# Layer two's last stage of a two-layer network on one core: where factor loads are issued, and how many places the squares have

## The chip, the core and the metric

The kernel runs on one core of a Trainium2 chip. TensorE multiplies, VectorE and ScalarE prepare its operands and empty its accumulators, and 16 DMA engines move data between HBM and the core's memory. Transfers are issued from two queues here: SyncE's (written SP) and ScalarE's (written ACT). The metric is device time of the whole program in microseconds (us), lower is better.

## What is computed

A causal attention with decaying weights feeds two layers; the change touches the last matrix product of the second layer.

```
x = attention(q, k, v)                     # 2304 tokens x 512
h1 = x @ w_in1;  g1 = elu(h1);  y = g1 @ w_out1
h2 = maximum(y @ w_in2, 0)                 # 2304 x 2048
out = (h2 * h2) @ w_out2                   # 2304 x 512
```

All weights arrive as 64-bit floats and everything must hold float32 accuracy. So each operand is split into a high and a low part, and each product is three matmuls (high by high, high by low, low by high).

## The kernel before, in words

Both products of layer two are done as Strassen-like products: the matrices are cut into 2x2 blocks, and seven block products replace eight. For `(h2*h2) @ w_out2` the seven combinations of the weight blocks, the **factors**, are made earlier in the program and parked in HBM (`wo2s`); the squares `h2*h2` are parked in HBM too (`g2s`).

The stage of the second product (`up2`, matmuls of line 492) works through steps numbered `i` = 0 to 23; its matmuls write accumulators A, B and D, ScalarE copies or squares them (lines 509, 570, 571), VectorE adds (lines 519, 522), and SyncE stores the squares (line 525).

The last stage (`down2`, matmuls of line 675) follows. Its unit is called a **set** here: for one column of 128 tokens per half (`u`, nine of them) and one pair of feature blocks (`jj`, four of them), it loads 512 KB of squares from `g2s` (line 637, queue SP), makes seven combinations out of them, splits each (a cast on ScalarE in line 159, a subtraction on VectorE in line 160; sums between blocks on VectorE in lines 659 and 662), and runs 7 products x 2 blocks x 3 = 42 matmuls. There are 36 sets, 1512 matmuls. The first call takes `u` = 0 and 1 by turns, so set 0 is (jj 0, u 0), set 1 is (jj 0, u 1), set 2 is (jj 1, u 0), set 3 is (jj 1, u 1), set 4 is (jj 2, u 0) and so on to set 7; after that four sets for each `u`.

The loaded squares go to the pool `raw`, three places of 512 KB, taken in rotation; the load of a set waits until the set three before it has been cast and summed. The split combinations `S` go to three places in rotation (two of pool `x`, one made of four tiles of pool `g`).

The factors come back from HBM in ten **groups** of six tiles, 1536 KB each (the tenth 512 KB), by `load_last` in line 615, issued from ScalarE's queue. The group takes the memory that the operands T of the second product held (tags `w0` to `w9`), so it waits until these are used. Groups 0 to 4 are issued after the steps that the dictionary in line 874 names, 5 to 9 in the first five passes of `down2`, right behind the issue of a set's load of squares (line 642). For the 42 matmuls of set 0 or 1 the groups 0 to 2 are needed, for sets 2 and 3 the groups 2 to 4, for sets 4 and 5 the groups 4 to 6, for sets 6 and 7 the groups 7 to 9; from then on all ten stay in memory.

What is issued on an engine follows an order that a scheduler makes with a model of times, starting from the order of the program; each engine's queue is then worked off strictly in that order. In the trace the sets' squares are tiles `g` (in the order below `g_7052` is set 0, `g_7111` set 1, `g_7170` set 2, `g_7232` set 3, `g_7291` set 4), and the groups are tiles `wo` (`wo_6957` is group 3, `wo_7023` group 4, `wo_7054` group 5, `wo_7113` group 6, `wo_7172` group 7, `wo_7234` group 8, `wo_7293` group 9).

Of the kernel before, what the change touches and what calls it, by code (L numbers as in the profile page):

```python
# [9 lines left out]
F32 = mybir.dt.float32  # L10
# [8 lines left out]
P = 128  # L19
# [53 lines left out]
def tokens(half, u):  # L73

    blk = max(b for b in range(NB) if COL0[b] <= u * P)
    t, n = BLOCKS[blk]
    return t + half * n // 2 + u * P - COL0[blk]
# [49 lines left out]
def tile_kernel(ctx: ExitStack, tc, q, k, v, w_in1, w_out1, w_in2, w_out2, cst, out):  # L127
# [3 lines left out]
    wp = pool("wp", 1)  # L131
    raw_p = pool("raw", 3)
# [24 lines left out]
    def split(pair_hi, pair_lo, src, eng=nc.vector):  # L157

        nc.scalar.copy(pair_hi, src)  # L159
        eng.tensor_tensor(out=pair_lo, in0=src, in1=pair_hi.bitcast(F32), op=ALU.subtract)  # L160
# [213 lines left out]
    def down(blk, f):  # L374
        n = BLOCKS[blk][1]
        g, w = g_t.pop((blk, f)), w_t[0, 1, f]
        shared = blk < 2
        first, last = (any(f == r[e] - (e == 1) for r in (GROUPS if shared else ((0, NF),))) for e in range(2))
        if first:
            acc_t[blk] = [ps_acc.tile([P, TB], F32, tag="acc", name=f"acc{m}") for m in range(KC)]  # L380

        back = shared and last and f >= GROUPS[0][1]
        end = last and f == NF - 1
        part = []
        for m in range(KC if last else 0):
            if end:
                if m % 2 == 0:
                    both = raw_p.tile([P, 2, TB], F32, tag="raw", name="x2")
                t = both[:, m % 2]
            else:  # L390
                t = n_p.tile([P, TB], F32, tag="qkv"[m % 3], name="part")
            part.append(t[:, :n])
            if back:
                nc.sync.dma_start(out=part[m], in_=parts[blk, :, m, :n])
        for m in range(KC):
            c = slice(m * P, (m + 1) * P)
            a = acc_t[blk][m][:, :n]
            mm3(a, w[:, 0, c], w[:, 1, c], g[:, 0, :n], g[:, 1, :n], first, last)
            if not last:
                continue  # L400
            if back:
                nc.vector.tensor_tensor(out=part[m], in0=a, in1=part[m], op=ALU.add)  # L402
            else:
                nc.scalar.copy(part[m], a)
            if not end:
                nc.sync.dma_start(out=parts[blk, :, m, :n], in_=part[m])
                continue
            for half in range(2):
                for j in range(n // 2 // P):
                    o = half * n // 2 + j * P  # L410
                    nc.sync.dma_start(
                        out=x2s[COL0[blk] // P + j][:, m // 2 * 2 + half, m % 2], in_=part[m][:, o:o + P]
                    )
# [197 lines left out]
    def load_last(g):  # L611
        t = wp.tile([P, 6, 2, DM // 2], F32R, tag=f"w{g}", name=f"wo{g}")
        n = min(6, 7 * HF - 6 * g)

        tc.keep_in_program_order(nc.scalar.dma_start(
            out=t.bitcast(F32)[:, :n].rearrange("p q a b -> p q (a b)"),
            in_=wo2s[6 * g:6 * g + n].rearrange("q p a b -> p q (a b)"),
        ))
        for i in range(n):
            wo_t[6 * g + i] = t[:, i]  # L620

    sets = [0]

    def down2(us, loads=()):

        loads = list(loads)
        banks = {}
        for i, u in enumerate(us):
            for k in range(4):
                ps, tag = ((ps_acc, "acc"), (ps_acc, "acc"), (ps_h, "h"), (ps_a, "a"))[k]  # L630
                banks[u, k] = ps.tile([P, 2, DM // 2], F32, tag=tag, name=f"m{k}")
        m = lambda u, k: banks[u, PLACE[k][0]][:, PLACE[k][1]]
        for jj in range(HF // 2):
            for u in us:
                c, s = divmod(u, NCH)
                r = raw_p.tile([P, 2, 4, P], F32, tag="raw", name="g2")
                nc.sync.dma_start(
                    out=r.rearrange("p j x c -> p j (x c)"),
                    in_=g2s[c][s, 2 * jj:2 * jj + 2].rearrange("j p a b c -> p j (a b c)"),
                )  # L640
                if loads:
                    load_last(loads.pop(0))

                if sets[0] % 3 < 2:
                    t = x_p.tile([P, 2, 2, 7, P], F32R, tag="x", name="S")
                    at_ = [t[:, :, :, o] for o in range(7)]
                    span = lambda o, n: t[:, :, :, o:o + n]
                else:
                    ts = [g_p.tile([P, 2, 2, 2, P], F32R, tag="g", name="S") for _ in range(4)]
                    at_ = [ts[(o + 1) // 2][:, :, :, (o + 1) % 2] for o in range(7)]  # L650
                    span = lambda o, n: ts[(o + 1) // 2][:, :, :, (o + 1) % 2:(o + 1) % 2 + n]
                sets[0] += 1
                a11, a21, a12, a22 = (r[:, :, i] for i in range(4))

                def put(o, n, src):
                    d = span(o, n)
                    split(d[:, :, 0], d[:, :, 1], src)

                sub = lambda out, x, y: nc.vector.tensor_tensor(out=out, in0=x, in1=y, op=ALU.subtract)  # L659
                put(0, 1, r[:, :, 0:1])  # L660
                put(1, 2, r[:, :, 2:4])
                nc.vector.tensor_tensor(out=a22, in0=a21, in1=a22, op=ALU.add)
                sub(a21, a11, a21)
                sub(a11, a22, a11)
                sub(a12, a12, a11)
                put(3, 2, r[:, :, 0:2])
                put(5, 2, r[:, :, 2:4])
                for k in (1, 2, 6, 7, 4, 5, 3):
                    for e in range(2):
                        j = 2 * jj + e  # L670
                        l, w = at_[ST[k - 1]][:, e], wo_t[7 * j + WT[k - 1]]
                        for i, (x, y) in enumerate(((0, 0), (0, 1), (1, 0))):

                            first = j == 0 and i == 0
                            ins = nc.tensor.matmul(  # L675
                                m(u, k), l[:, x], w[:, y], start=first and k in (1, 6, 4, 5), stop=j == HF - 1 and i == 2,
                                skip_group_check=True,
                            )
                            if first:
                                tc.stamp_issue_order_token(ins.ins, f"bank{u}_{PLACE[k][0]}")  # L680
        for u in us:
            c1 = n_p.tile([P, DM], F32, tag="q", name="c1")
            v = n_p.tile([P, DM], F32, tag="k", name="v")
            o = [n_p.tile([P, 2, DM // 2], F32, tag="v", name=f"o{h}") for h in range(2)]
            c1, u2, u3 = c1[:, :DM // 2], v[:, :DM // 2], v[:, DM // 2:]
            add = lambda out, x, y: nc.vector.tensor_tensor(out=out, in0=x, in1=y, op=ALU.add)
            nc.scalar.copy(c1, m(u, 1))
            add(o[0][:, 0], m(u, 2), c1)
            add(u2, m(u, 6), c1)
            add(u3, m(u, 7), u2)  # L690
            add(o[1][:, 0], m(u, 4), u3)
            add(o[1][:, 1], m(u, 5), u3)
            add(u2, m(u, 5), u2)
            add(o[0][:, 1], m(u, 3), u2)
            for h in (1, 0):
                t0 = tokens(h, u)
                nc.sync.dma_start(out=out[t0:t0 + P, :], in_=o[h].rearrange("p a b -> p (a b)"))
# [154 lines left out]
    def expand(n):  # L852
        make(n)
        first, *rest = made[n]
        queue[0:0] = rest + [lambda: make(n + 1)]
        first()

    for i, (f, c) in enumerate(seq):
        now = up2(f, c)
        for n, (at_, _) in enumerate(tasks):  # L860
            if at_ == i:
                if i in (5, 18):
                    queue.extend([lambda: None] * 2)
                queue.append(lambda n=n: expand(n))
        for k in TURNS.get(i, (1, 5, 7, 2, 6, 4, 3)):
            whose = last if k in (7, 4) else now
            if whose:
                whose[k]()
            if k in (7, 4) and pend:
                down(*pend.pop(0))  # L870
            between()
        last = now

        for g in {20: (0,), 21: (1, 2), 22: (3,), 23: (4,)}.get(i, ()):
            load_last(g)
    while queue:
        queue.pop(0)()
    last[7]()
    last[4]()
    down2((0, 1), (5, 6, 7, 8, 9))  # L880
    for u in range(2, NU):
        down2((u,))

# [25 lines left out]
```

## Time and profile before

| | us |
|---|---|
| median of 3 runs | 890.87 |
| lowest and highest run | 886.36, 891.96 |
| profiled execution, whole time | 890.54 |
| its span (first to last instruction) | 888.7 |
| TensorE busy in the span | 857.8 (97%) |
| VectorE, ScalarE busy | 685.7, 490.6 |

The three runs lie 5.6 us apart, so one run says little about a few us. The profiled execution lies 0.33 us under the median, with 1.84 us around its span. All times of single instructions below come from this one execution, counted from the start of the span; the last stage runs from about 696 to 885.

### The profile page before, as it was taken

The page shows a single profiled execution, that of the slowest core. Times are in us where ns is not written, and L with a number is a line of the kernel's source. Part 1 is how long each engine was busy: PE and PEld are TensorE (multiplying, and loading weights), DVE is VectorE, ACT ScalarE, POOL GpSimd, SP SyncE. Part 2 cuts the span into 40 slices and gives each one's busy share as a digit, 9 for nine tenths or more (in the row PEclk, how much of TensorE's full clock was granted, in tenths as well). Part 3 has the DMA queues.
Part 4 walks back from the last instruction along what each step waited for, and adds up shares of the span by engine and source line. Part 5 has one row for each costly group of instructions (what it writes and reads, how often), then busy time and mean ns, then how long its engine had stood idle before and what let it go on. Part 6 is the DMA issues. An engine that isn't in the chain of part 4 may idle for free.

```text
span 888.7 us, 14956 instructions
## 1 busy us (share of the span) xinstructions
PE 857.8 (97%) x5630; PEld 771.3 (87%) x5630; DVE 685.7 (77%) x1391; ACT 490.6 (55%) x961; POOL 8.7 (1%) x12
## 2 busy tenths in 40 slices
PE   7898999999998999999999999999999989999998
PEld 5686888888887988888888898999989989999997
DVE  4998888885666868766778867789884769898984
ACT  3674778673464656555767744556553434444441
POOL 3000000000000000000000000000000000000000
PEclk9999899999999999999999999999999999999999
DMA  9944306383529656533462034499998994444330
GB/s 226 276 107 160 96 24 190 119 214 95 142 63 221 163 157 185 187 107 131 142 225 95 25 104 157 154 328 332 348 319 281 401 345 137 160 146 144 120 131 37
DMA packets 157608, 155.33 MB, mean 175 GB/s; under 512 B 62816, under 2 KB 121312, under 8 KB 157536
## 3 DMA queue, kind: packets, MB, share of 16 engines
q1 hardware_dynamic: 150208, 139.69, 51.9%
q10 hardware_dynamic: 7328, 14.68, 4.6%
q8 instruction: 44, 0.72, 0.3%
q14 instruction: 28, 0.23, 0.1%
HBM read 98.77 MB, written 55.57 MB: 174 GB/s over the span
## 4 chain that ended last, share of the span: by engine, by line
PE 73%; DVE 10%; DMA 9%; issue 3%; ACT 2%; SPq 2%; ACTq 0%; DVEq 0%
PE m L675 18%; PE acc L163 7%; PE acc L164 7%; PE acc L165 7%; PE h L163 7%; PE h L164 6%; PE h L165 6%; PE A L492 5%; PE D L492 3%; DMA k<-in_k_dram 2%; DMA f<-w2s 2%; PE ps_o L325 2%; DVE go L519 1%; DMA wo2s<-wo 1%; PE ps_o L321 1%
## 5 line engine op out<-in xcount | busy, mean ns | idle before, releaser
L675 PE MATMUL m<-wo,S 128*128 128x256 f32 x1512 | 183.8, 284 | 3.6 <-ACT S L159 3.6
L675 PEld LDWEIGHTS m<-wo,S 128*128 128x128 f32 x1512 | 183.3, 193 | 4.0 <-ACT S L159 4.0
L159 ACT CAST S<-g 128x512 fp32r<-128x512 f32 (+1 forms) x144 | 75.3, 565 | 94.2 <-DVE g L659 45.6
L163 PE MATMUL h<-x,w 128*128 128x512 f32 (+1 forms) x320 | 120.3, 378 | 3.4 <-DVE t L370 2.4
L165 PE MATMUL h<-x,w 128*128 128x512 f32 (+1 forms) x320 | 118.8, 371 | 0.0
L164 PE MATMUL h<-x,w 128*128 128x512 f32 (+1 forms) x320 | 118.7, 371 | 0.0
L164 PE MATMUL acc<-g,w 128*128 128x512 f32 (+1 forms) x320 | 118.5, 371 | 0.0
L165 PE MATMUL acc<-g,w 128*128 128x512 f32 (+1 forms) x320 | 117.5, 370 | 0.0
L492 PE MATMUL A<-T,pair 128*128 128x384 f32 x576 | 113.4, 336 | 1.5 <-DVE go L519 0.8
L163 PE MATMUL acc<-g,w 128*128 128x512 f32 (+1 forms) x320 | 111.4, 375 | 2.2 <-DVE x L402 1.3
L492 PEld LDWEIGHTS A<-T,pair 128*128 128x128 f32 x576 | 100.5, 188 | 4.0 <-DVE go L519 2.3
L160 DVE TENSOR_TENSOR S<-g,S 128x512 fp32r<-128x512 f32 (+1 forms) x144 | 86.4, 621 | 22.7 <-ACT S L159 20.9
L365 ACT ACTIVATE t<-h 128x512 f32<-128x512 f32 (+1 forms) x80 | 44.3, 554 | 82.5 <-PE h L165 78.9
L369 DVE SCALAR_TENSOR_TENSOR t<-e,t 128x512 f32<-128x512 f32 (+1 forms) x80 | 50.8, 635 | 49.3 <-ACT t L367 49.0
L163 PEld LDWEIGHTS h<-x,w 128*128 128x128 f32 x320 | 60.6, 190 | 15.5 <-DVE t L370 3.4
L159 ACT CAST g<-t 128x512 fp32r<-128x512 f32 (+1 forms) x80 | 46.2, 578 | 47.0 <-DVE t L370 45.2
L163 PEld LDWEIGHTS acc<-g,w 128*128 128x128 f32 x320 | 59.4, 188 | 13.4 <-DVE x L402 1.7
L165 PEld LDWEIGHTS h<-x,w 128*128 128x128 f32 x320 | 60.7, 190 | 10.6 <-DVE w L160 0.2
L164 PEld LDWEIGHTS h<-x,w 128*128 128x128 f32 x320 | 60.7, 190 | 10.2
L164 PEld LDWEIGHTS acc<-g,w 128*128 128x128 f32 x320 | 60.3, 188 | 10.2
L165 PEld LDWEIGHTS acc<-g,w 128*128 128x128 f32 x320 | 60.2, 188 | 10.1
L492 PE MATMUL D<-T,pair 128*128 128x384 f32 x288 | 58.5, 336 | 1.7 <-DVE pair L160 1.1
(88 smaller groups left out, 1279.3 us busy)
## 6 DMA issues: line engine op xcount, KB each, us to landing
g2s<-go SPq DMA_DIRECT2D x48, 384.0 KB, 4.4
g<-g2s SPq DMA_DIRECT2D x36, 512.0 KB, 3.7
raw<-in_moe_w_in_dram SPq DMA_DIRECT2D x32, 512.0 KB, 5.6
raw<-in_moe_w_out_dram SPq DMA_DIRECT2D x32, 512.0 KB, 4.3
wo2s<-wo SPq DMA_DIRECT2D x56, 256.0 KB, 4.2
wo<-wo2s ACTq DMA_DIRECT2D x9, 1536.0 KB, 14.8
w2s<-f SPq DMA_DIRECT2D x32, 256.0 KB, 2.2
f<-w2s SPq DMA_DIRECT2D x32, 256.0 KB, 3.9
```

Of the source, the lines that this page charges most:

```text
L159: nc.scalar.copy(pair_hi, src)
L160: eng.tensor_tensor(out=pair_lo, in0=src, in1=pair_hi.bitcast(F32), op=ALU.subtract)
L163: nc.tensor.matmul(ps, l_hi, r_hi, start=first, stop=False)
L164: nc.tensor.matmul(ps, l_hi, r_lo, start=False, stop=False)
L165: nc.tensor.matmul(ps, l_lo, r_hi, start=False, stop=last)
L321: i = nc.tensor.matmul(ps[:, p, :n], st[:, p, :], qT[:, p, :n], start=p == 0, stop=True, skip_group_check=True)
L325: nc.tensor.matmul(ps[e * D:(e + 1) * D, p, :n], vn[:n, 2 * p + e, :], live[e][:n, p, :n], start=not s, stop=True, skip_group_check=True,)
L365: nc.scalar.activation(t, h, AF.Relu, scale=-1.0)
L369: nc.vector.scalar_tensor_tensor(out=t, in0=e, scalar=1.0, in1=t, op0=ALU.add, op1=ALU.mult)
L492: ins = nc.tensor.matmul(ps, w[:, l, o:o + P], t[:, r, j], start=first and i + j == 0, stop=i + j == 3, skip_group_check=True)
L519: nc.vector.tensor_tensor(out=out, in0=by3(x), in1=by3(y), op=ALU.add)
L675: ins = nc.tensor.matmul(m(u, k), l[:, x], w[:, y], start=first and k in (1, 6, 4, 5), stop=j == HF - 1 and i == 2, skip_group_check=True,)
```

## The change

There are three edits. The squares of the last stage get two more places of 512 KB: sets are numbered by fives, and the fourth and fifth of each five share one tile of the tag `w10`, which held the operand T of the seventh product until the second product's end; the first three rotate over `raw` as ever. The issue of a factor group in the first passes of `down2` moves from behind the load of the set's squares to behind the set's last cast. And group 4 is issued one step earlier (after step 22 with group 3), group 5 after step 23, so that `down2` issues four groups and not five.

```diff
     sets = [0]
+    spots = []
+
+    def next_squares():
+
+        n = sets[0] % 5
+        if n < 3:
+            return raw_p.tile([P, 2, 4, P], F32, tag="raw", name="g2")
+        if n == 3:
+            spots[0:] = [wp.tile([P, 2, 2, 4, P], F32, tag="w10", name="g2")]
+        return spots[0][:, n - 3]
 
     def down2(us, loads=()):
...
-                r = raw_p.tile([P, 2, 4, P], F32, tag="raw", name="g2")
+                r = next_squares()
                 nc.sync.dma_start(
...
                 )
-                if loads:
-                    load_last(loads.pop(0))
-
                 if sets[0] % 3 < 2:
...
                 put(3, 2, r[:, :, 0:2])
                 put(5, 2, r[:, :, 2:4])
+                if loads:
+                    load_last(loads.pop(0))
                 for k in (1, 2, 6, 7, 4, 5, 3):
...
-        for g in {20: (0,), 21: (1, 2), 22: (3,), 23: (4,)}.get(i, ()):
+        for g in {20: (0,), 21: (1, 2), 22: (3, 4), 23: (5,)}.get(i, ()):
             load_last(g)
...
-    down2((0, 1), (5, 6, 7, 8, 9))
+    down2((0, 1), (6, 7, 8, 9))
```

The scheduler makes another order of this. Up to the issue of group 3 every engine's order is the same as before. ScalarE's queue at steps 22 and 23 before (`wo_6957` is group 3, `wo_7023` group 4; the lines 509, 570 and 571 belong to step 23):

```order
L615 DMA wo_6957<-wo2s 128x6x512
L509 COPY c_6966<-A 128x384
L509 COPY m_6975<-D 128x384
L509 COPY u_7002<-A 128x384
L570 ACTIVATE t<-A 128x384
L159 CAST S<-g_7052 128x2x128
L159 CAST S<-g_7052 128x2x256
L571 ACTIVATE go<-t 128x3x128
L615 DMA wo_7023<-wo2s 128x6x512
```

The same place after the change, where groups 4, 5 and 6 are `wo_6959`, `wo_7025` and `wo_7069`, and set 0 is `g_7054`:

```order
L615 DMA wo_6957<-wo2s 128x6x512
L615 DMA wo_6959<-wo2s 128x6x512
L509 COPY c_6968<-A 128x384
L509 COPY m_6977<-D 128x384
L509 COPY u_7004<-A 128x384
L570 ACTIVATE t<-A 128x384
L159 CAST S<-g_7054 128x2x128
L159 CAST S<-g_7054 128x2x256
L571 ACTIVATE go<-t 128x3x128
L615 DMA wo_7025<-wo2s 128x6x512
L159 CAST S<-g_7054 128x2x256 x2
L615 DMA wo_7069<-wo2s 128x6x512
```

Group 4 is now issued directly behind group 3, ahead of step 23's copies, and groups 5 and 6 in the order of their numbers, where before group 6 (`wo_7113`) went ahead of group 5 (`wo_7054`). ScalarE's queue a little later before, from group 5 to the first casts of set 4 (`g_7291`):

```order
L615 DMA wo_7054<-wo2s 128x6x512
L159 CAST S<-g_7170 128x2x256
L159 CAST S<-g_7111 128x2x256 x2
L615 DMA wo_7172<-wo2s 128x6x512
L159 CAST S<-g_7170 128x2x256 x2
L615 DMA wo_7234<-wo2s 128x6x512
L159 CAST S<-g_7232 128x2x128
L159 CAST S<-g_7232 128x2x256 x3
L615 DMA wo_7293<-wo2s 128x2x512
L159 CAST S<-g_7291 128x2x128
L159 CAST S<-g_7291 128x2x256 x3
```

And after, from the last casts of set 1 (`g_7113`) on; set 2 is `g_7172`, the tile of sets 3 and 4 together is `g_7234`, and groups 7, 8 and 9 are `wo_7128`, `wo_7190` and `wo_7249`:

```order
L159 CAST S<-g_7113 128x2x256 x2
L615 DMA wo_7128<-wo2s 128x6x512
L159 CAST S<-g_7172 128x2x256 x2
L159 CAST S<-g_7234 128x2x128
L159 CAST S<-g_7234 128x2x256
L159 CAST S<-g_7172 128x2x256
L615 DMA wo_7190<-wo2s 128x6x512
L159 CAST S<-g_7234 128x2x128
L159 CAST S<-g_7234 128x2x256 x3
L615 DMA wo_7249<-wo2s 128x2x512
L159 CAST S<-g_7234 128x2x256 x2
```

The second cast of set 2 now stands behind the issue of group 7 and no longer ahead of it, and the issue of group 9 stands ahead of the second half of set 4's casts, where it stood ahead of the first half.

SyncE's queue before, around the first loads of squares that wait for a place:

```order
L525 DMA g2s_106<-go 128x3x256 x3
L637 DMA g_7232<-g2s_104 128x2x512
L525 DMA g2s_106<-go 128x3x256
L637 DMA g_7291<-g2s_104 128x2x512
L637 DMA g_7350<-g2s_104 128x2x512
```

And after:

```order
L525 DMA g2s_106<-go 128x3x256 x2
L647 DMA g_7234<-g2s_104 128x2x512 x2
L525 DMA g2s_106<-go 128x3x256
L647 DMA g_7349<-g2s_104 128x2x512
L525 DMA g2s_106<-go 128x3x256
```

The loads of sets 3 and 4 now stand together, ahead of the last two stores of squares. On TensorE the first matmul that needs the last of the groups 0 to 6 to be issued has 171 of the stage's matmuls ahead of it before (it needs `wo_7054`, group 5, here with three rows ahead of it):

```order
L675 MATMUL m_7050<-wo_6891,S 128x256 x3
L675 MATMUL m_7050<-wo_6957,S 128x256 x3
L675 MATMUL m_7044<-wo_7023,S 128x256 x3
L675 MATMUL m_7044<-wo_7054,S 128x256 x3
L675 MATMUL m_7044<-wo_7023,S 128x256 x2
```

and 172 after (it needs `wo_7069`, group 6); ten matmuls of set 3 (accumulator `m_7052`) now stand behind it:

```order
L684 MATMUL m_7051<-wo_6959,S 128x256 x3
L684 MATMUL m_7047<-wo_7025,S 128x256 x2
L684 MATMUL m_7046<-wo_7069,S 128x256 x3
L684 MATMUL m_7049<-wo_7069,S 128x256 x3
L684 MATMUL m_7052<-wo_6891,S 128x256
```

So seven groups have to be there at practically the same matmul as before.

## Rows read from the trace of the kernel before

**Rows 1.** The page: span, and the last stage's matmuls among the costliest groups.

```profile
span 888.7 us, 14956 instructions
...
L675 PE MATMUL m<-wo,S 128*128 128x256 f32 x1512 | 183.8, 284 | 3.6 <-ACT S L159 3.6
```

**Rows 2.** Who waited for whom, TensorE and its weight loads, last stage (total, times, longest).

```profile
PE m L675 <- ACT S L159: 3.6, 2, 3.0
...
PEld m L675 <- ACT S L159: 4.0, 2, 3.3
```

**Rows 3.** The chain that ended last, 684 to the end (start, us, what).

```profile
700.87 9.32 DMA g<-g2s
...
714.42 6.38 issue
...
721.33 163.09 PE m L675 x1344
```

**Rows 4.** Timeline, 687 to 800 (start, us, engine, line; in brackets idle time before).

```profile
687.46 0.37 ACTq L615 DMA_DIRECT2D wo<-wo2s  x1
...
689.01 0.48 ACT L509 COPY c<-A 128x384 f32<-128x384 f32 x1 [1.03 <-PE A L492]
...
691.93 2.24 PE L492 MATMUL A<-T,pair 128*128 128x384 f32 x12
...
698.95 0.51 PE L675 MATMUL m<-wo,S 128*128 128x256 f32 x2 [0.55 <-ACT S L159]
...
700.38 17.91 PE L675 MATMUL m<-wo,S 128*128 128x256 f32 x148
...
704.49 3.05 ACTq L615 DMA_DIRECT2D wo<-wo2s  x1
...
707.64 0.62 ACT L159 CAST S<-g 128x512 fp32r<-128x512 f32 x1 [2.05 <-DVE g L659]
...
708.11 1.54 ACTq L615 DMA_DIRECT2D wo<-wo2s  x1
...
713.74 7.02 ACTq L615 DMA_DIRECT2D wo<-wo2s  x1
...
721.33 18.76 PEld L675 LDWEIGHTS m<-wo,S 128*128 128x128 f32 x143 [3.25 <-ACT S L159]
...
727.84 72.25 PEld L675 LDWEIGHTS m<-wo,S 128*128 128x128 f32 x601
```

**Rows 5.** Factor groups 4, 6 and 5: issue, and time from issue to landing.

```profile
L615 ACTq DMA_DIRECT2D wo<-wo2s x1: 366/366/366, 694.7 to 694.7; - x1
DMA to landing us min/median/max: 11.8/11.8/11.8
...
L615 ACTq DMA_DIRECT2D wo<-wo2s x1: 366/366/366, 698.7 to 698.7; - x1
DMA to landing us min/median/max: 14.8/14.8/14.8
...
L615 ACTq DMA_DIRECT2D wo<-wo2s x1: 366/366/366, 701.1 to 701.1; - x1
DMA to landing us min/median/max: 19.5/19.5/19.5
```

**Rows 6.** Stretches: engines' busy time, TensorE's granted clock, DMA share, GB/s.

```profile
700.00:704.00 4.00, 4.00 (x35) 4.00 (x34) 3.57 (x8) 1.80 (x5) 0.00 (x0) 1.00 1.06 401
...
720.00:724.00 4.00, 2.67 (x12) 2.67 (x13) 2.45 (x6) 0.99 (x3) 0.00 (x0) 0.66 1.05 387
...
740.00:760.00 20.00, 20.00 (x169) 20.00 (x168) 18.69 (x46) 8.53 (x17) 0.00 (x0) 1.00 0.50 167
760.00:800.00 40.00, 40.00 (x335) 40.00 (x335) 36.43 (x85) 18.99 (x37) 0.00 (x0) 1.00 0.45 145
```

**Rows 7.** The load of set 4's squares: issue, and time to landing.

```profile
L637 SPq DMA_DIRECT2D g<-g2s x1: 360/360/360, 706.8 to 706.8; - x1
DMA to landing us min/median/max: 9.0/9.0/9.0
```

## The prediction

> **What bounds the kernel now.** I read the page first: TensorE is busy 97% of the span, and in the last stage its 1512 matmuls sat idle for only 3.6 us [rows 1]. The view of waits names two waits, both for casts of line 159, 3.6 us on the matmuls and 4.0 us on the weight loads, the longest 3.0 and 3.3 [rows 2]. So whatever the change does right in the matmuls' order, the waits that it can take away come to 4 us of 891. The chain of waits then shows where the long one comes from: a load of squares (9.32 us), then 6.38 us of "issue" at 714.4, then TensorE without a break from 721.33 to the end, 1344 matmuls [rows 3]. The timeline gives that "issue" its name: at 713.74 ScalarE's queue took 7.02 us to issue the last factor group, and the casts of set 4 stood behind it [rows 4]. TensorE had run dry at 700.38 + 17.91 = 718.29 (20 + 148 matmuls, which are the 168 of sets 0 to 3), and went on at 721.33.
>
> The wait has a second cost. After it the granted clock is 0.66 in the stretch 720 to 724 (a mix of the levels 1.2 and 2.4 GHz), where it had been 1.00 [rows 6]. The 143 weight loads after the wait took 18.76 us, 0.1312 each; the 601 behind them took 72.25, 0.1202 each [rows 4]. The difference is 143 x 0.011 = 1.6 us. All that the stage can give back is therefore 4.0 + 1.6 = 5.6 us, of which the shorter wait, 0.55 to 0.7 us at 698.95, hangs on set 0's second casts, whose place the change leaves alone. That leaves 3.3 + 1.6 = 4.9.
>
> But the cast is not the only thing that came late. Group 5 was issued at 701.1 and landed 19.5 us later, at 720.6 [rows 5], and the order shows that set 4 needs it three matmuls after its start (behind 171 matmuls). Had the casts been ready at 718.3, TensorE would still have waited until 720.6; the cast cost only 721.33 - 720.6 = 0.73 us beyond the data. The question is thus when the seventh factor group lands.
>
> **Groups 4 and 5 a step sooner.** Group 4 would be issued at about 687.9 behind group 3 (687.46, [rows 4]), not at 694.7. Yet the groups land in the order of issue: 4 at 694.7 + 11.8 = 706.5, 6 at 698.7 + 14.8 = 713.5, 5 at 720.6 [rows 5], each about 7 us behind the one ahead although the issues were 4.0 and 2.4 us apart. The queue always had work, and the DMA engines moved 401 GB/s at a share of 1.06 [rows 6]. Issuing sooner puts a transfer into a queue that is already full; it doesn't move its landing. I count nothing for it. What the edit does change is the order of 5 and 6: group 5 becomes the sixth to land (at about 713.5), 6 the seventh (about 720.6). TensorE needs group 6 behind 172 matmuls, where it needed the seventh group behind 171. The bound stays where it was.
>
> The Trainium skill, "DMA: Bandwidth & Descriptors", section "Issuing engines are not separate DMA queues", speaks against this edit: transfers from all issuing engines run on the same 16 DMA engines, and issuing concurrently saves only the sequencer's time, usually little. By that rule an earlier issue gives nothing; by a constant time from issue to landing (11.8 us) group 4 would land at 699.7. The spacing of the landings agrees with the rule.
>
> **Two more places for squares.** Set 4's load, issued at 706.8, landed at 715.8 [rows 7], set 3's at 710.2 [rows 3]. Now both are issued at about 696.5, when the seventh product of step 23 has let go of `w10`, and I expect them to land at 705 to 709. That is a gain for their casts, but what they move comes out of the same 401 GB/s: at most one load of 524 kB more before the seventh group lands, 524 / 401 = 1.3 us. The bounds are 0 (it is moved from later in the same full stretch) and +1.3; I take +0.6, the middle, since part of these loads ran before 720 anyway.
>
> **Issues behind the casts.** Every issue of a factor group that found three groups still open was held in ScalarE's queue: 3.05 us at 704.49 (4, 6 and 5 open), 1.54 at 708.11, 7.02 at 713.74; at 694.7, 698.7 and 701.1 two were open and the issue took 0.37 [rows 4, 5]. After the change groups 4, 5 and 6 each find three open. A hold costs only through what stands behind it. Behind group 4's stands the copy of line 509 (689.01, 0.48 us), which TensorE needs at 691.93: a slack of 691.93 - 689.49 = 2.4 us [rows 4]. Behind group 6's stand set 1's first casts, behind group 7's set 2's second cast. These can make TensorE wait here and there before matmul 172. The waits are free as long as they sum to less than 720.6 - (718.29 + 4 x 0.121) = 1.8 us, since it would wait for the data anyway. Behind group 9's issue stands the second half of set 4's casts, needed behind 170 matmuls. In the trace the hold ended at 720.76, 0.16 after the seventh landing, and one cast later TensorE ran; the same now gives 0.16 + 0.62 (a 128x512 cast [rows 4]) + 0.1 = 0.9 us after the landing, against 0.73 before. So TensorE is past matmul 172 between 720.6 (casts there in time) and 720.6 + 1.3 + 0.9 = 722.8, where at full clock it was at 721.33 + 4 x 0.121 = 721.8 before. That is -1.2 to +1.0 us; with +0.6 and 0.9 it is 722.1, +0.3.
>
> **The clock.** The one wait of 3.0 us now falls into several: one where set 2's second cast is late behind group 7's issue, one at matmul 170, and smaller ones between. After waits of 1 us and less the rows give 1.00 (the 0.55 at 698.95 lies just before the stretch 700 to 704 [rows 4, 6]). I take it that the clock now stays, and 1.6 us come back; if the last wait is still about 3 us, none does.
>
> **The rest of the stage** is bound by TensorE, and nothing of its work changes: 1340 matmuls at 0.1202. The sum against the profiled execution's own 890.54 is +0.3 - 1.6 = -1.3. It lies 0.33 under the median, so I forecast 890.87 - 1.3 = 889.6.
>
> **The rivals.**
>
> First, sooner issue does land sooner, and the long wait goes altogether with its clock: -4.9, which is 886.0. For it: the change moves group 4 by 6.9 us, and at 698 to 700 the queue of stores might leave room. Against it: the spacing of landings and 401 GB/s. Chance 0.10.
>
> Second, on the slower side: the held issues. Group 4's issue now finds three groups open. If its hold lasts like the longest (7.02), the copy ends at 687.9 + 7.0 + 0.5 = 695.4, and TensorE waits 695.4 - 691.9 = 3.5 us in the second product, with a clock fall of its own (1.6). Group 7's issue, with set 2's second cast now behind it, adds 1.5 to 3.1 as its like did, middle 2.3. Then TensorE reaches matmul 172 at 718.8 + 3.5 + 1.6 + 2.3 = 726.2, 4.4 us later than at 721.8, and only the old clock loss of 1.6 is saved: +2.8, which is 893.7. It decides from a hold of 2.4 us on group 4, or from waits of more than 1.8 us in all before matmul 172. For it: all three issues that found three groups open were held. Against: two of the three holds (3.05 and 1.54) would eat at most a little of the slack. Chance 0.20.
>
> Third, the steady part suffers: two sets share one tile, so the load of the fourth set of five waits for both, and VectorE, with 18.69 of 20 us busy from 740 to 760 and 36.43 of 40 after that [rows 6], has little room if the new order makes it wait. Seven such pairs at 1 us each give +7, 897.9. Against it: no wait of TensorE there before, and five places instead of three. Chance 0.06.
>
> That the seventh landing binds wholly and the clock falls as before, so that nothing changes (890.9), I count with the forecast; together 0.64.
>
> **How the numbers follow.** The likeliest is 889.6. The range goes from the first rival to the second, 885.5 to 894.0, and leaves out the third and a little at the ends. A measurement of this kernel can tell about 1% (8.9 us) from no change. Faster by more than that asks for under 882, beyond all that the stage can give: 0.02. Slower by more asks for over 899.8, the third rival at its worst: 0.04. Within 1%: 0.94.
>
> **What the profile after would show.** If I am right: the factor groups' landings still 5 to 7 us apart, group 4 from issue to landing 18 to 20 us and not 11.8, the seventh landing at 720 to 722; set 4's squares landing before 710; a held issue at group 4 and again at the last group; TensorE's waits in the last stage still 2 to 5 us in sum but in several pieces; a clock of 1.00 from 716 to 728; TensorE without a break from about 730 on. I am wrong on the bound if the seventh group lands before 718, wrong on the clock if it falls again around 720, and wrong on the cost if TensorE waits in the second product between 690 and 696 or anywhere after 735.

## The result, and the profile of the changed kernel

The changed kernel took 895.79 us, median of five runs (894.86 to 896.82), the kernel before 889.96 on the same chip (886.36 to 891.96): a ratio of 1.0076, 95% interval 1.0053 to 1.0099. On a second chip the ratio was 1.0041 (1.0022 to 1.0059). It is slower, by some 4 to 7 us; 889.6 was forecast.

The profiled execution is the one of 895.79 us, with a span of 893.9. Two parts of it have to be kept apart. The stage's first matmul comes at 697.63 instead of 696.09: 1.5 us that arise ahead of the changed code, since group 3's issue, up to which both kernels have the same order on every engine, is already as late (689.00 instead of 687.46). In the first 50 us the granted clock is 0.90 here and 0.97 in the profile of before; among all the kernels below the stage begins anywhere between 691.8 and 699.0. The changed stage itself goes from 697.63 to 889.66, 192.03 us, where it went from 696.09 to 884.42, 188.33. The change costs 3.7 us in this execution, and the stage's length is what is compared from here on.

The view of waits, for TensorE's matmuls, its weight loads, and ScalarE (total, times, longest):

```profile
PE m L684 <- ACT S L159: 6.5, 2, 5.9
...
PEld m L684 <- ACT S L159: 7.5, 5, 6.1
...
ACT S L159 <- DMA wo<-wo2s: 8.4, 1, 8.4
```

There are still two waits of the matmuls, for the same line as in [rows 2], but the longest is 5.9 us and no longer 3.0. The third row is new: a cast on ScalarE that waited 8.4 us for the landing of a **factor group**. A cast reads squares, not factors, so it can't have needed that data. Something ahead of it in ScalarE's queue did. The chain that ended last (start, us, what) answers to [rows 3]:

```profile
689.40 19.47 DMA wo<-wo2s
...
708.90 0.37 ACTq L615
...
709.82 2.53 PE m L684 x10
712.35 1.61 PE A L492 x6
...
716.12 173.54 PE m L684 x1444
```

The chain runs from a group's transfer (issued at 689.40, landed at 708.88) to the *issue of another group* at 708.90, on to set 1's first casts, and from there to TensorE. In [rows 3] it came from a load of squares. The timeline of the same place (idle time before in brackets; rows of before in [rows 4]):

```profile
689.00 2.47 ACTq L615 DMA_DIRECT2D wo<-wo2s  x2
...
691.51 0.48 ACT L509 COPY c<-A 128x384 f32<-128x384 f32 x1 [1.99 <-PE A L492]
...
696.28 0.74 ACTq L615 DMA_DIRECT2D wo<-wo2s  x1
...
700.49 3.40 PE L684 MATMUL m<-wo,S 128*128 128x256 f32 x24 [0.55 <-ACT S L159]
...
708.90 0.37 ACTq L615 DMA_DIRECT2D wo<-wo2s  x1
709.36 1.23 ACT L159 CAST S<-g 128x256 fp32r<-128x256 f32 x3 [8.40 <-DMA wo<-wo2s]
...
709.82 2.53 PE L684 MATMUL m<-wo,S 128*128 128x256 f32 x10 [5.93 <-ACT S L159]
```

Groups 3 and 4 are issued together, group 5 at 696.28, group 6 not before 708.90. The issue itself then takes 0.37 us: it was not held in a full queue, it had not been allowed to begin. The program's listing of ScalarE's queue says why. It names the semaphores that each row waits for; these are the counters on which engines and transfers report what they have done:

```
L615 DMA wo_6959<-wo2s 128x6x512 [waits DMAHW0_49]
...
L615 DMA wo_7025<-wo2s 128x6x512 [waits DMAHW3_49]
L159 CAST S<-g_7054 128x2x256 [waits DVE_49] x2
L615 DMA wo_7069<-wo2s 128x6x512 [waits DMAHW0_49]
L159 CAST S<-g_7113 128x2x128 [waits DVE_49,PE_49]
```

The transfers of SyncE's and ScalarE's queues report their end on eight semaphores, DMAHW0 to DMAHW7, given out in turn. Group 4 (`wo_6959`) reports on DMAHW0; two stores, group 5, a store, two loads of squares and a store lie between; group 6 (`wo_7069`) is the eighth behind it, gets DMAHW0 again, and may start only when group 4 has landed. In the kernel before, the row of the group in this place, `wo_7113`, carries no wait for a transfer at all. The pattern was there all the same: its group 5 (`wo_7054`) is the eighth transfer behind group 3 and waits for that group's semaphore, DMAHW7. Group 3 landed at 700.63 and group 5 was issued at 701.11, so it cost nothing. ScalarE takes its rows in order, so in the changed kernel set 1's first casts (`g_7113`) stand behind the wait.

Group 4 and group 6, from issue to landing, to be read against [rows 5]:

```profile
L615 ACTq DMA_DIRECT2D wo<-wo2s x1: 2067/2067/2067, 689.4 to 689.4; - x1
DMA to landing us min/median/max: 19.5/19.5/19.5
...
L615 ACTq DMA_DIRECT2D wo<-wo2s x1: 367/367/367, 708.9 to 708.9; - x1
DMA to landing us min/median/max: 12.1/12.1/12.1
```

Group 6, the seventh to land, is there at 721.0; the seventh landed at 720.6 before. TensorE comes to the matmul that needs it (172 ahead of it) only at 728.7, so this landing no longer holds anything up. The bandwidth was not lost (402 GB/s while TensorE stood still), only ScalarE's time. The stretches, as in [rows 6]:

```profile
704.00:708.00 4.00, 0.00 (x0) 0.00 (x0) 0.00 (x0) 0.00 (x0) 0.00 (x0) 0.83 1.05 402
708.00:712.00 4.00, 2.18 (x10) 2.19 (x11) 2.20 (x5) 1.23 (x3) 0.00 (x0) 0.50 1.06 394
712.00:716.00 4.00, 4.00 (x24) 3.73 (x23) 2.03 (x6) 1.98 (x4) 0.00 (x0) 0.82 1.06 396
716.00:720.00 4.00, 3.98 (x33) 3.88 (x33) 3.64 (x8) 1.79 (x5) 0.00 (x0) 1.00 1.05 389
```

From 704 to 708 nothing computes, and from 708 to 712 the granted clock is 0.50, the lower level of 1.2 GHz. After 716.12 TensorE doesn't stop again. The account of the stage: the new wait 5.93 and its slow stretch 1.4 (from 709.82 to 713.79 for 10 + 6 matmuls, 3.97 us, against 2.57 for the same in the experiment with a tiny transfer below, at full clock); against the old wait 3.05 and its slow stretch 1.6, both gone. That is +2.7. Short waits of weight loads that were not there before (7.5 - 0.75 - 6.1) add 0.6. Of the 3.7 some 0.4 stay unassigned.

### The profile page after: what moved, and what is told of

The parts are those of the page before. It is cut to its first block, busy times and chain, and to the rows that moved or that the text cites. A ratio compares the mean times of both kernels' runs of the same rounds, so it can differ in the third digit from the quotient of the medians.

```text
span 893.9 us, 14954 instructions
## 1 busy us (share of the span) xinstructions
PE 862.0 (96%) x5630; PEld 774.9 (87%) x5630; DVE 686.1 (77%) x1391; ACT 490.2 (55%) x961; POOL 8.9 (1%) x12
## 4 chain that ended last, share of the span: by engine, by line
PE 77%; DMA 9%; DVE 8%; issue 2%; SPq 2%; ACT 2%; POOL 0%; ACTq 0%; DVEq 0%
PE m L684 20%; PE acc L163 7%; PE acc L164 7%; PE acc L165 7%; PE h L163 7%; PE h L165 7%; PE h L164 6%; PE A L492 5%; PE D L492 3%; DMA wo<-wo2s 2%; PE ps_o L325 2%; DMA wo2s<-wo 2%; PE ps_o L321 1%; PE ps_s L306 1%; DMA f<-w2s 1%
```

## The experiments

Three theories. **A**: the loss is the wait of group 6's issue for group 4's landing, with set 1's casts behind it. **B**: it is the other kind of hold, which the prediction knew, a queue with three groups open. **C**: one of the edits costs by itself: the place of the issues behind the casts, or the two more places for squares (C': by the bytes that their loads put ahead of the factor groups).

The table has each kernel's stage (first matmul to last, from its one profiled execution), the landing of group 8 (after the stage's first matmul; counted from group 0 it is the ninth group, where some expectations below say the eighth), and the ratio of timed runs to before on the same chip. Three kernels were profiled twice. Their stages differ by 0.7 to 1.9 us between the two executions and their landings by at most 0.7, so a difference of 1 us between two stages decides nothing by itself.

| kernel | stage, us | group 8 lands | ratio (95%) |
|---|---|---|---|
| before | 188.3 | +33.5 | 1 |
| changed | 192.0 | +34.6 | 1.0076 (1.0053 to 1.0099) |
| changed, another chip | 192.8 | +34.6 | 1.0041 (1.0022 to 1.0059) |
| changed + one tiny transfer | 190.3 | +38.1 | 1.0026 (1.0005 to 1.0048) |
| the same again | 191.0 | +38.7 | 1.0011 (0.9989 to 1.0032) |
| changed, issues ahead of the casts | 193.6 | +34.5 | 1.0043 (1.0018 to 1.0068) |
| changed, issues from set 1 on | 188.7 | +39.0 | 1.0041 (1.0018 to 1.0064) |
| the same again | 190.6 | +39.4 | 1.0022 (1.0000 to 1.0044) |
| changed, three places | 188.1 | +33.9 | 1.0007 (0.9986 to 1.0028) |
| three places, issues from set 1 on | 188.1 | +35.0 | 0.9986 (0.9969 to 1.0002) |
| before + two more places | 190.8 | +37.3 | 1.0014 (0.9999 to 1.0029) |
| before + groups 4, 5 sooner | 192.3 | +31.5 | 1.0033 (1.0010 to 1.0055) |
| before + issues behind casts | 188.4 | +35.3 | 0.9991 (0.9975 to 1.0006) |
| three places + two tiny transfers | 189.8 | not in the trace | 1.0009 (0.9994 to 1.0024) |
| three places + three tiny transfers | 190.2 | +33.8 | 1.0036 (1.0017 to 1.0055) |
| three places + two idle loads + one tiny | 192.2 | +36.1 | 1.0047 (1.0031 to 1.0064) |

**The changed kernel again**, beside the single edits on the second chip:

> The changed kernel unaltered, beside its single edits on one chip. Both theories: slower than before by 0.4 to 0.8 per cent (893 to 897), with the 8 us wait of ScalarE's queue for group 4's landing and TensorE's wait of 5.9 us for set 1's casts in the same place again.

Both waits come again, and a little longer:

```profile
PE m L684 <- ACT S L159: 7.0, 2, 6.4
...
ACT S L159 <- DMA wo<-wo2s: 8.9, 1, 8.9
```

The stage is 192.8 us, and the ratio 1.0041. The loss is there on another chip, in the same place.

**One tiny transfer.** 32 bytes in SyncE's queue between group 4 and group 6, in the changed kernel, so that group 6 is the ninth transfer behind group 4 and no longer the eighth:

```
+    tick = dram.tile([1, 8], F32, tag="tick", name="tick")
...
             load_last(g)
+            if g == 5:
+                for _ in range(1):
+                    tc.keep_in_program_order(nc.sync.dma_start(out=tick, in_=wo2s[0, :1, 0, :8]))
```

> The changed kernel with one tiny transfer (32 bytes, DRAM to DRAM) put into SyncE's queue between the issue of group 4 and that of group 6. All else stays in its place; group 6's issue then no longer waits for group 4's landing (it takes another completion semaphore). Theory A (that wait is the loss): the 8.4 us of ScalarE's queue before set 1's casts shrink to a hold of 0.4 to 3 us, TensorE's wait of 5.9 us for them goes, it waits for the seventh landing near 720.6 instead, and the time is that of the kernel before, 889 to 891.5. Theory B (it is the queue with three groups open that holds the issue): the hold stays over 5 us, 894 to 897. Theory C (the place of the issues behind the casts, or the two more places, costs by itself): 894 to 897 with the wait gone.

Its timeline (lines are one higher than in the changed kernel):

```profile
700.07 1.82 ACTq L616 DMA_DIRECT2D wo<-wo2s  x1
...
704.17 1.68 PE L685 MATMUL m<-wo,S 128*128 128x256 f32 x10 [0.49 <-ACT S L160]
...
722.44 10.81 PE L685 MATMUL m<-wo,S 128*128 128x256 f32 x88 [0.87 <-ACT S L160]
735.53 152.21 PE L685 MATMUL m<-wo,S 128*128 128x256 f32 x1254 [2.28 <-DMA wo<-wo2s]
```

Group 6 is issued at 700.07 (it was 708.90) and held 1.82 us; the wait for set 1's casts falls from 5.93 to 0.49. Thirty-two bytes that nobody reads take 8.4 us out of ScalarE's queue: the cause of the wait is shown, and theory B, which wanted a hold of over 5 us, is out. The wait itself has not gone from the chip. The tiny transfer has DMAHW0 now, and SyncE's queue, free from 702.0 on, stands before it until group 4 has landed:

```profile
701.64 0.36 SPq L526 DMA_DIRECT2D g2s<-go  x1
708.50 0.76 SPq L888 DMA_DIRECT2D tick<-wo2s  x1
709.37 0.37 SPq L648 DMA_DIRECT2D g<-g2s  x1
```

Behind it stands the load of set 5's squares, issued at 702.44 in the changed kernel; it lands 19.6 us after the stage's first matmul in both, so there the wait costs nothing. Yet the stage falls only to 190.3. TensorE now waits elsewhere: 2.28 us at 735.5 for group 8, which landed at 38 us and not at 34. So A is right on the wait and was wrong that nothing else is late. The timed runs alone would hardly show the gain: the interval of 1.0026 overlaps the changed kernel's on the second chip.

**Three places.** The changed kernel with its squares in three places again; groups 4 and 5 sooner and issues behind the casts stay:

```
-                r = next_squares()
+                r = raw_p.tile([P, 2, 4, P], F32, tag="raw", name="g2")
```

> The changed kernel without the two more places for squares (three places, as before); groups 4 and 5 a step sooner and issues behind the casts stay. With fewer loads between them, group 6's issue comes six transfers after group 4's and waits for a store's completion, not for group 4. Theory A (wait for group 4's landing): no long hold before set 1's casts, 889 to 891.5. Theory B (three open groups hold the issue): hold over 5 us as in the changed kernel, 894 to 897. Theory C, if it is the places' loads that cost: 889 to 891.5 as well; if it is the issues' place behind the casts: 894 to 897.

Stage 188.1, that of before. With two loads fewer between them, group 6's issue is the sixth transfer behind group 4 and waits for a store that has long ended. No wait of its matmuls is over 0.78 us:

```profile
705.80 1.68 PE L674 MATMUL m<-wo,S 128*128 128x256 f32 x10 [0.49 <-ACT S L159]
...
725.90 6.31 PE L674 MATMUL m<-wo,S 128*128 128x256 f32 x47 [0.64 <-ACT S L159]
732.99 1.70 PE L674 MATMUL m<-wo,S 128*128 128x256 f32 x12 [0.78 <-DMA wo<-wo2s]
734.87 152.30 PE L674 MATMUL m<-wo,S 128*128 128x256 f32 x1267 [0.18 <-DMA wo<-wo2s]
```

The two more places, then, bring the whole loss in company of the other two edits. This kernel alone can't tell whether by the wait or by their loads.

**Issues ahead of the casts.** The changed kernel with the issues where they were before:

```
                 )
+                if loads:
+                    load_last(loads.pop(0))
...
-                if loads:
-                    load_last(loads.pop(0))
```

> The changed kernel with the factor loads issued where they were before (behind a set's load, not behind its casts); two more places and groups 4 and 5 a step sooner stay. The first issue of the stage still comes eight transfers after group 4's and waits for its landing. Theory A: ScalarE's queue again stands about 8 us before set 1's casts, TensorE waits about 6 us, 894.5 to 897. Theory B: the same. Theory C, if the place behind the casts costs: 889 to 891.5.

Stage 193.6. Its waits repeat those of the changed kernel to 0.1 us:

```profile
ACT S L159 <- DMA wo<-wo2s: 8.4, 1, 8.4
```

The place behind the casts, which the prediction argued about most, is not what costs. (That the stage is even 0.8 to 1.6 us longer than in the changed kernel's two executions is not explained here.) The listing shows the first issue of the stage (here it is group 7) with the same wait for DMAHW0 in the same row of the queue.

**Issues from set 1 on.** The changed kernel, but set 0 issues no group, so set 1's casts stand ahead of the first issue:

```
-                if loads:
+                if loads and sets[0] > 1:
                     load_last(loads.pop(0))
```

> The changed kernel, but set 0 issues no factor group: groups 6 to 9 are issued behind the casts of sets 1 to 4, so set 1's casts stand ahead of group 6's issue, which also no longer waits for a factor group. Theory A: no long hold, TensorE runs to matmul 172 and waits there for the seventh landing, which comes at 720 to 723 since group 6 is issued at about 704: 889 to 892. Theory B: the same, with holds of 1.5 to 7 us behind which only later casts stand. Theory C (places): 894 to 897.

The stage took 188.7 us, as A wanted, and TensorE's one long wait was 3.23 us for group 8, at 39.0. But the timed runs lay 0.4% above before, which 188.7 does not explain; the profiled execution, 886.82 us, was the shortest of the twelve, whose median is 892.67. It was executed again, with this said beforehand:

> The kernel with issues from set 1 on, a second execution. If the fall of the clock after its wait for the eighth group comes and goes: the stage takes 190 us or more from its first matmul when the clock falls, 188.7 when it doesn't, and the timed runs lie 1 to 3.5 us above before. If the first timing was chance: stage 188.5 to 189, 889 to 891.

The same matmuls behind the same wait, in the first and in the second execution:

```profile
731.05 149.65 PE L684 MATMUL m<-wo,S 128*128 128x256 f32 x1245 [3.23 <-DMA wo<-wo2s]
```

```profile
734.73 151.15 PE L684 MATMUL m<-wo,S 128*128 128x256 f32 x1245 [3.67 <-DMA wo<-wo2s]
```

And the stretches of the second, around the wait's end:

```profile
732.00:736.00 4.00, 1.27 (x6) 1.27 (x7) 0.49 (x1) 0.00 (x0) 0.00 (x0) 0.85 0.99 364
736.00:740.00 4.00, 4.00 (x27) 4.00 (x27) 2.42 (x6) 1.20 (x3) 0.00 (x0) 0.72 0.11 40
```

In the first execution both stretches have a clock of 1.00. The fall of the clock after a wait comes and goes in one and the same kernel, and 149.65 against 151.15 us for 1245 matmuls is its price: 1.50 us. With it and a wait longer by 0.44 us the stage is 190.6, near that of the kernel with one tiny transfer, which was executed again too:

> The changed kernel with one tiny transfer, a second execution: the wait for group 4's landing stays gone. Stage 190 us with a fall of the clock after the wait for the eighth group, 188.7 without; 890 to 893.

190.3 and 191.0 us, both with a fall of the clock (0.61 and 0.74 in the stretches after the wait for group 8).

**Three places, issues from set 1 on.** The kernel with issues from set 1 on, without its two more places. The edit takes away the places alone; the scheduler's order and the semaphores change with it:

> Groups 4 and 5 a step sooner, three places, issues behind the casts, and set 0 issues none, so that groups 6 to 9 go behind the casts of sets 1 to 4. Theory A: nothing long stands ahead of set 1's casts; but group 6 is issued 8 us later, and if the queue runs short of work it lands later than 23 us after the first matmul. Even with it: 887.5 to 889.5 if the issues' holds were what is left to gain; 889.5 to 892 if the landing binds.

Stage 188.1, ratio 0.9986 (0.9969 to 1.0002): faster than the changed kernel, not to be told from the kernel before. Group 6 is again the eighth transfer behind group 4 here, and its row waits for DMAHW0; but set 1's casts stand ahead of it, group 4 landed at 702.99, and the issue came at 703.29, so the same row cost nothing further back in the queue. Beside its sister with five places it shows what the places' loads do. What the queues moved from group 3's issue to group 8's landing (SyncE's queue is q1; loads of squares are `g<-g2s`), here, with three places:

```profile
q1 hardware_dynamic: 4137, 5.53, 34.9%
...
g<-g2s SPq DMA_DIRECT2D x6, 512.0 KB, 8.3
```

and with five:

```profile
q1 hardware_dynamic: 4945, 7.10, 41.1%
...
g<-g2s SPq DMA_DIRECT2D x10, 512.0 KB, 8.8
```

Four loads more are issued in that time, 1.57 MB more are moved, and at the 395 GB/s of the stretch that is 4.0 us. Group 8 lands at 39.0 instead of 35.0 us. That agrees with C', by the megabyte. It is an account of the delay and no separate proof: group 8 was also issued later with five places (21.9 us after the first matmul against 19.2), and no run here adds the bytes and nothing else.

**Single edits on the kernel before.** The two more places alone; groups 4 and 5 sooner alone; issues behind the casts alone (the diffs are the three parts of the change):

> The kernel before with the two more places alone. Its first issue of the stage now comes after group 3's landing (it reuses group 3's completion semaphore), which is due about 2 us after that issue. Theory A (only the long wait for a factor landing costs): a hold of 2 to 3 us there, not 8; TensorE waits 0 to 1.5 us more for set 1's or 2's casts; 889.5 to 891.5. Theory C (the extra loads of squares go ahead of the factor groups and delay them by 1.3 us each): TensorE waits 1.3 to 2.6 us more for the seventh or eighth group, 891 to 893.5.

> The kernel before with groups 4 and 5 a step sooner alone; the issues stay behind a set's load, and by the order group 7 is then issued ahead of group 6, whose issue waits for group 4's landing. Theory A (late issues cost by what stands behind them): that wait is 1 to 4 us long, since the issue stands later than in the changed kernel; but group 6 is the eighth to land, at 725 to 728, and TensorE, which needs it behind 172 matmuls, waits for it: 892 to 895. If the landing doesn't bind: 889 to 891.

> The kernel before with the issues moved behind the casts alone. By the order no issue waits for a factor group that is still open, and the groups go in the order 4, 5, 6, 7. Theory A: no long hold, TensorE waits for the seventh landing near 721 as before or for casts behind a held issue, 888.5 to 891. Theory C (the place behind the casts costs by itself): 892 to 896.

Places alone: stage 190.8. The wait for group 3's landing came, with 1.5 us on ScalarE where 2 to 3 were expected; TensorE's 4.20 us were not expected, and came from the last group's issue. Sooner alone: stage 192.3, the expected time by another way. Group 6 was issued at 708.46, 0.02 us after group 4's landing, and ScalarE lost nothing of note to that wait, where 1 to 4 us were expected; TensorE did not wait for group 6 but, again, for casts behind the last group's issue:

```profile
714.09 6.78 ACTq L615 DMA_DIRECT2D wo<-wo2s  x1
...
721.65 168.81 PE L675 MATMUL m<-wo,S 128*128 128x256 f32 x1386 [3.93 <-ACT S L159]
```

With places alone that hold is 7.39 us (710.42), in the kernel before 7.02 [rows 4]. Theory B's hold exists, then, and costs TensorE 3 to 4.2 us where the next set's casts stand behind it; it is not what happened in the changed kernel. Behind alone: no hold over 0.71 us, stage 188.4, ratio 0.9991. Moving the issues behind the casts does what it looks like it should, and TensorE waits 2.48 us for group 8 in exchange.

**Tiny transfers in ScalarE's queue.** To put the wait back without the places, two transfers of 32 bytes behind group 5 in the kernel with three places make group 6 the eighth behind group 4; three make it the ninth:

```
+    for t in tick:
+        tc.keep_in_program_order(nc.scalar.dma_start(out=t, in_=wo2s[0, :1, 0, :8]))
     while queue:
```

> The kernel without the two more places, with two tiny transfers (32 bytes each) issued in ScalarE's queue right behind group 5, so that the first issue of the stage, group 6's, is again the eighth transfer after group 4's and waits for its landing. No byte that matters is added and no place. Theory A (that wait costs): the 8 us wait of ScalarE's queue and TensorE's wait of about 6 us for set 1's casts come back, the stage takes 192 to 193 us from its first matmul, 892.5 to 896. If the wait were harmless and only the places' loads cost: 888.5 to 891, stage 188 to 189.

> The same with three tiny transfers: one more of 32 bytes, and group 6's issue is the ninth after group 4's and no longer waits for its landing. Theory A: no long hold, stage 188 to 189.5, 888.5 to 891.5. If it were the tiny transfers in ScalarE's queue that cost: as with two, or slower.

This pair missed. ScalarE's waits with two:

```profile
ACT S L160 <- DMA wo<-wo2s: 5.9, 2, 5.2
ACT S L160 <- DMA tick<-wo2s: 4.5, 1, 4.5
```

The wait for group 4 came back, but shorter (5.2 us), since ScalarE had already stood 4.5 us at the tiny transfers; TensorE waited 2.69 us for set 0's second casts and 1.62 for set 1's. With three, ScalarE stood 5.7 us at them, with set 0's casts behind: 3.92 us of TensorE. In both the long part is theory B's hold, with three groups open: the first tiny transfer's issue took 3.35 us of two and 4.41 of three. The third has group 3's semaphore, but was issued 0.12 us after the second was done. All three together:

```profile
693.23 5.75 ACTq L877 DMA_DIRECT2D tick<-wo2s  x3
```

So the control carried a hold of its own, and the pair does not separate what it was made for. What it does show: TensorE's waits for casts, 4.3 and 4.4 us early in the stage against 1.0 with three places alone, lengthen it by 1.7 and 2.1 us only (189.8 and 190.2 against 188.1), and TensorE then no longer waits for the later groups: after 712 it has no wait in either.

**Idle loads.** Three places, and two loads of squares of 524 kB that nobody reads where the two more places had theirs, with one tiny transfer against group 6's wait:

```
+                if sets[0] == 4:
+                    idle_load(0)
```

> The kernel without the two more places, but with two loads of squares of 524 kB, of which nothing is read, issued where the two more places had theirs, and the one tiny transfer that keeps group 6's issue from waiting for group 4. Theory C' (the places cost by the bytes that they put ahead of the factor groups, 1.3 us each at 401 GB/s): the eighth group lands 2 to 4 us later after the stage's first matmul than without them (36.5 to 38 us), TensorE waits for it, stage 190 to 192, 890.5 to 893. If bytes cost nothing: stage 188 to 189, 888.5 to 891.

Stage 192.2, group 8 at 36.1. This run missed too. TensorE did not wait for group 8 but for casts (its weight loads 7.7 us in 12 pieces), and ScalarE waited 19.1 us for loads of squares. SyncE's queue:

```profile
699.34 0.36 SPq L526 DMA_DIRECT2D g2s<-go  x1
706.36 0.76 SPq L886 DMA_DIRECT2D tick<-wo2s  x1
707.23 0.36 SPq L644 DMA_DIRECT2D g<-g2s  x1
```

As in its first kernel the tiny transfer holds SyncE's queue for group 4's landing, and here set 3's load stands behind it, issued 13.5 us after the stage's first matmul; with three places alone it was 4.2. So the run does not tell what bytes cost by themselves.

## Why the prediction was wrong, step by step

**What bounds the kernel now**: right for the kernel before, not for the changed one. The old wait of 3.05 us is gone, its slow stretch with it, and the seventh group landed at 721.0 where 720 to 722 was forecast. But that landing was taken for the bound, and TensorE came to it 7.7 us later, held up by casts.

**Groups 4 and 5 a step sooner**: right as a step. Group 4 took 19.5 us from issue to landing (18 to 20 forecast) and landed 11.2 us after the stage's first matmul, where it was 10.4 before, so sooner issue bought nothing. The Trainium skill's "DMA: Bandwidth & Descriptors", section "Issuing engines are not separate DMA queues", says that the transfers of all issuing engines run on the same 16 DMA engines, and that issuing from several at once saves only the time of issuing. It speaks of several engines and not of an earlier issue on one; group 4's landing is in line with it. Group 4's issue was held 2.07 us, inside the slack of 2.4; the copy came at 691.51 and TensorE did not wait.

**Two more places for squares**: mis-sized. Sets 3 and 4 were in at 707.5 and 710.2 (705 to 709 forecast, in a stage that began 1.5 us later). The price was put at one load (0 to 1.3 us). In the kernels where nothing holds ScalarE up it is four loads and 4.0 us on group 8's landing. The stage is longer by 0.6 us without a fall of the clock, less than two executions of one kernel differ, and by 2.2 to 2.9 with it (188.7, and 190.3 to 191.0, against 188.1 with three places). A place did not bring one load forward, it brought every later load forward. In the changed kernel itself this is hidden: the casts came so late that only seven loads went out before group 8, which landed at 34.6.

**Issues behind the casts**: this is the step that failed. It asked how long an issue is held by a full queue, found 1.5 to 3.1 us in the rows of before, and allowed the casts behind it 1.8 us in sum before anything was lost; the casts behind group 6's issue it therefore put at nothing. TensorE's wait for them was 5.9 us, and it was of another kind: the issue waited for the end of the transfer eight places ahead, because it reports on the same semaphore. The profile of before has no long wait of this kind, though its group 5 waits for group 3 in the same way; the listing of the changed kernel's queue, read with its waits, shows it. It is not the place behind the casts (moved back: 193.6) but the other two edits together: with groups 4 and 5 sooner and three places the first issue of the stage is the sixth transfer behind group 4, and the two loads more of the five places make it the eighth. The hold that was forecast at the last group's issue did not come (0.37 us).

**The clock**: wrong. It was to stay at 1.00 since the one long wait would fall into short ones. The wait became longer, and the clock fell to 0.50.

**The rest of the stage**: right; TensorE has no wait from 716 on, and the third rival (five places hurting the steady part) is out.

The second rival, held issues, had the side and the point of decision right, over 1.8 us of waits before matmul 172, but not the cause: it looked for holds by a full queue, at group 4's copy and behind group 7, and stopped at 893.7. Of the 895.79 measured, 1.5 us come from that execution's late start of the stage, outside the change; the second chip's median is 893.02, 2.75 above its own before.

Open: how the loss of the changed kernel would divide had only one of its two causes been there. Taking the wait out of ScalarE's queue leaves 190.3 to 191.0, and taking the places out leaves 188.1; the first cause hides the second, so their prices don't add. That the places cost by their bytes, and not by the later issue of group 8, is argued from the sums and not shown by a run. Why the clock falls after a wait of 2.3 us in one kernel and not after one of 3.2 in another is open too.

## What to carry to other kernels

Before moving a transfer, list each queue with the semaphores that its rows wait for, and look at what an *issue* waits for, not only at what the data feeds: with eight completion semaphores in turn, an issue can wait for a big transfer eight places ahead, and everything behind it on that engine waits along. Count bytes, not places, where the transfer engines are full: a further buffer brings all later loads forward, and they take their time from whatever lands last. When two causes of lateness lie in a row, taking one away shows the other, so test the edits in pairs and compare the stage's own length, since here its start moved by 7 us although the code ahead of it was the same. And ask of a control what it waits for itself: the tiny transfers here brought a wait or a hold of their own each time.

## What was not expected of the hardware

A transfer of 32 bytes took a wait of 8.4 us out of ScalarE's queue, by its place in the round of eight semaphores alone, and SyncE's queue waited 6.5 us in its stead at no cost. The clock's fall after a wait comes and goes: in the same kernel the granted clock stayed at 1.00 after a wait of 3.23 us and fell to 0.72 after one of 3.67; it also fell after 2.28 and stayed after 2.48 in two other kernels. And one issue took 7.39 us where three groups were open, as in the kernel before, for a transfer of a third of a group's size.
